# A fused attention and feed-forward kernel on one core: blocks of eight key tiles, three feed-forward banks, weight parts kept in memory

## The chip, the cores and the metric

The kernel runs on one core of one Trainium2 chip. The time is device microseconds (us) of one execution. A core has TensorE (PE: matmuls, with a queue for loading weights, PEld), VectorE (DVE), ScalarE (ACT), GpSimd (POOL) and SyncE (SP), whose queue issues most DMAs here. Matmuls write to eight PSUM banks of 128 x 512 fp32; DVE and ACT read them.

## The reference

Input x has 2048 tokens of 512 features; everything is fp32.

```python
xn = _layernorm(x, axis=-1)
s = _A_ref(xn, A_wqkv, A_wo)                          # 32 heads of 16: softmax(q k^T / 4) v, then @ wo
g = _silu(_B_ref(xn, B_w_gate, B_w_up, B_w_down))     # (silu(xn @ w_gate) * (xn @ w_up)) @ w_down, width 1792
return x + s * g
```

## The kernel before

**Precision.** Most matmuls use an fp32 operand split into a high and a low part of a rounded fp32 type (hi, then the rest), and three products of parts (high x high, high x low, low x high) stand for one. DVE makes the parts: a copy into the rounded type, then a subtraction.

**Stages.** A prologue normalises and transposes x, projects q, k and v for all heads and writes them to memory (`q_d`, `k_d`, `v_d`); the transposed input goes to `xt_d`. Then comes the attention stage, in which two streams of matmuls are woven together on PE:

- *Attention.* 32 units (a group of 4 heads times a quarter of the queries, 512), each with 16 key tiles of 128 keys. For a key tile there are two score pairs: two heads at a time, on the upper and lower 64 rows of PE at once, each to its own bank. ACT takes the exponential of the scores from PSUM into a tile `pr`. Then `values()` multiplies the exponentials with v, four heads side by side, into the bank `acc`. The units are cut into blocks of 2 to 6 key tiles. In block n the score pairs of block n are issued, with the values of block n - 1 in one run after its first two pairs.
- *Feed-forward* (`ffn`), in quarters of 512 tokens: 14 column tiles of gate and up ("gated tiles", 24 passes each), in two groups of seven; after a group, four token tiles of the down projection, 3 passes for each member of the group. `both()` issues a pass: two half-height matmuls at once, the upper 64 rows into `bankx`, the lower into `banky`. `fill(n)` issues the next n passes; the main loop calls it after every score pair, so that PE has work while ACT works on the scores.
- After the feed-forward the projection by `wo` (`project_out`) is issued by the same `fill`.

**PSUM.** `bankx`, `banky`, `acc`, two double banks `score` (a pair of heads each, emptied by one 128 x 1024 exponential) and one `spare`. The last pair of a block, and some pairs named in `SHARED`, put their second head into `spare`; there one half is emptied by a DVE copy (a *drain*), to be taken through the exponential from SBUF after the block's other exponentials (`kept_back`), or both by ACT one after the other.

**Order.** The order of every engine's instructions is that of the program text (manual schedule); `plan()` chooses sizes of blocks and numbers of passes after each score pair by a search over costs. Engines wait for each other by semaphores. All weight DMAs stand in SP's queue: every quarter loads gate, up and down weights anew (`load_gu`, `load_wd`) and splits them on DVE (`split_gu`, `split_wd`). `load_fx` replaces the transposed input of a quarter, 4.2 MB with both parts, after the last gated tile of the quarter before.

The lines that matter: the score matmuls L899 and their exponentials L902 and L910, drains L907, exponentials from SBUF L920, values L423, feed-forward passes L237, splits L198, L199, L208 and L209, reload of `fx` L215.

Of the kernel before, what the change touches and what calls it, by code (L numbers as in the profile page):

```python
# [22 lines left out]
H = 32  # L23
# [9 lines left out]
GROUPS = (slice(0, 7), slice(7, NF))  # L33
FG = 7
# [7 lines left out]
SIZES = (2, 3, 4, 5, 6)  # L42
LAST = (3, 3, 3, 3, 2, 2)
FIRST = (4, 1, 4, 0, 4, 1, 2, 4, 4)
EARLY = 2


SHARED = {
# [3 lines left out]
}  # L52
# [5 lines left out]
def plan():  # L58

    ends = [0]
    for i in range(2 * NB):
        nf = GROUPS[i % 2].stop - GROUPS[i % 2].start
        for n in [3 * DC] * nf + [3 * nf] * NT:
            ends.append(ends[-1] + n)

    ends = [n - ends[1] for n in ends[2:]]
    first = [(4, ends[0])]
    units = H // 4 * NB
    start, stop = sum(k for k, _ in first), (units - 2) * KT
    pace = (ends[-1] - ends[0]) / (stop - start)
    short = lambda k, n: 15 * len(SHARED[k, n][0]) if (k, n) in SHARED else 250 * max(0, 6 * (k - 1) - n)
    ways = {at: {} for at in range(start, stop + 1)}
    ways[start][ends[0]] = 0, None
    for at in range(start, stop):
        room = KT - at % KT  # L80
        for done, (cost, _) in ways[at].items():
            rem = next((n for n in ends if n > done), done) - done
            for k in SIZES:
                for n in [rem] + list(range(3, rem - 2)):
                    to = at + k, done + n
                    if not n or n > 6 * k + 6 or k > room or room - k == 1:
                        continue
                    if abs(to[1] - ends[0] - (to[0] - start) * pace) > 45:
                        continue
                    c = cost + 327 + short(k, n) + (650 if n == rem and k == 2 else 0) + abs(n - 4.1 * k) / 2  # L90
                    if to[1] not in ways[to[0]] or ways[to[0]][to[1]][0] > c:
                        ways[to[0]][to[1]] = c, (at, done, k, n)

    rest = [3 * (DT - 1)] * EARLY
    pairs = {4: (2, 2), 5: (3, 2), 6: (3, 3)}
    cost = lambda r: ways[stop - r][ends[-1]][0] + sum(short(k, n) for k, n in zip(pairs[r], rest))
    r = min((r for r in pairs if ends[-1] in ways[stop - r]), key=cost)
    middle, step = [], ways[stop - r][ends[-1]][1]
    while step:
        middle.insert(0, step[2:])  # L100
        step = ways[step[0]][step[1]][1]
    rest += [3 * DT] * (NT * (NB - 1))
    parts = []
    for k, n in first + middle + list(zip(pairs[r] + 2 * LAST, rest)):
        m = 2 * k - 2
        even = [n // m + (i < n % m) for i in range(m)]
        shared, behind = SHARED.get((k, n), ((), even))
        parts.append((k, shared, [0, 0, *behind]))
    parts[0] = 4, (), list(FIRST[1:])
    return parts  # L110
# [3 lines left out]
def tile_block(ctx: ExitStack, tc: tile.TileContext, x, wqkv, wo, w_gate, w_up, w_down, out):  # L114
# [3 lines left out]
    mm, act, dve, sp, pool = nc.tensor.matmul, nc.scalar.activation, nc.vector, nc.sync, nc.gpsimd  # L118
# [8 lines left out]
    o_d = dram.tile([DT, NB, P, TB], F32, name="o_d")  # L127
    s_d = dram.tile([1, TB], F32, name="s_d")
# [10 lines left out]
    banks = (bankx, banky)  # L139
# [45 lines left out]


    def load_gu(i):
        f = i % NF
        raw = two.tile([P, DC, P], F32, tag="gur", name="gur")
        for j, w in enumerate((w_gate, w_up)):  # L190
            sp.dma_start(raw[j * HALF:(j + 1) * HALF], w[:, f * P:(f + 1) * P].rearrange("(c p) f -> p c f", p=HALF))
        gu[i] = [raw]

    def split_gu(i):
        raw = gu[i][0]
        hi = two.tile([P, DC, P], F32R, tag="guh", name="guh")
        lo = two.tile([P, DC, P], F32R, tag="gul", name="gul")
        dve.tensor_copy(hi, raw)  # L198
        dve.tensor_sub(lo, raw, hi.bitcast(F32))  # L199
        gu[i] = (hi, lo)  # L200

    def load_wd(i):
        raw = one.tile([P, D], F32, tag="wdr", name="wdr")
        sp.dma_start(raw, w_down[(i % NF) * P:(i % NF + 1) * P])
        wdr[i] = raw

    def split_wd(f, i):
        dve.tensor_copy(wd[:, f, 0], wdr[i])  # L208
        dve.tensor_sub(wd[:, f, 1], wdr[i], wd[:, f, 0].bitcast(F32))  # L209
# [15 lines left out]
    kept, waiting = [], []  # L225

    def split_hidden():
        while kept:
            f, ga = kept.pop(0)
            dve.tensor_copy(hh[:, f, 0], ga)  # L230
            dve.tensor_sub(hh[:, f, 1], ga, hh[:, f, 0].bitcast(F32))  # L231

    halves = [slice(h * HALF, (h + 1) * HALF) for h in range(2)]

    def both(lhs, rhs, start, stop):
        for bank, h in zip(banks, halves):
            mm(bank, lhs[h], rhs[h], start=start, stop=stop)  # L237

    def store_gate(y, r):
        th = one.tile([P, D], F32, tag="th", name="th")  # L240
        act(th, y, AF.Tanh, scale=0.5)
        dve.scalar_tensor_tensor(y, th, 1.0, y, op0=ALU.add, op1=ALU.mult)
        pool.dma_start(g_d[r:r + P], y)


    def ffn(b):
        for grp, part in enumerate(GROUPS):
            nf = part.stop - part.start
            for f in range(nf):
                i = b * NF + part.start + f  # L250
                if i + 1 < NB * NF:
                    split_gu(i + 1)
                if i + 2 < NB * NF:
                    load_gu(i + 2)
                hi, lo = gu.pop(i)
                n = 0
                for c in range(DC):
                    for wt, j in ((hi, 0), (hi, 1), (lo, 0)):
                        both(wt[:, c], fx[:, j, c], n == 0, n == 3 * DC - 1)
                        n += 1  # L260
                        if n == 3 * DC:
                            th = one.tile([P, TB], F32, tag="th", name="th")
                            ga = two.tile([P, TB], F32, tag="ga", name="ga")
                            act(th, bankx, AF.Tanh, scale=0.5)  # L264
                            dve.scalar_tensor_tensor(ga, th, 1.0, bankx, op0=ALU.add, op1=ALU.mult)  # L265
                            dve.scalar_tensor_tensor(ga, ga, 0.5, banky, op0=ALU.mult, op1=ALU.mult)
                            kept.append((f, ga))
                            waiting.append((f, i))
                            if now >= 0:
                                split_hidden()  # L270
                            if grp == 1 and f == nf - 1 and b + 1 < NB:
                                load_fx(b + 1, 0)
                                load_fx(b + 1, 1)
# [39 lines left out]
    def next_out(t):  # L313
# [3 lines left out]
        if t + 1 < DT:  # L317
            load_wo(t + 1)
# [698 lines left out]
```

## Time and profile before

| | |
|---|---|
| runs shown | 1396.76 and 1397.27 us, median 1397.01 |
| profiled execution: span, first to last instruction | 1394.9 us |
| PE / ACT / DVE busy in it | 1388.4 / 1108.9 / 689.8 us |
| first score to last values | 157.6 to 1382.7 us |
| exponentials: 128 x 1024 / 128 x 512 from PSUM / from SBUF | 743 / 336 / 226 |
| DMA | 149.16 MB, mean 107 GB/s |

What lies around the span is the difference of 2.1 us between it and the median. In the profile a row of the timeline is: start, length, engine, line, operation, out<-in, count, and in brackets the idle time before it with what ended it. L12 is line 12 of the kernel. Matmuls overlap and their ends are modelled, so the distance between starts is read, not the length.

### The profile page before, as it was taken

Reading aid. Unit: us, or ns where it says so; the run is one execution under the profiler, and the core shown is the slowest. Engines: PE = TensorE matmul, PEld = TensorE weight load, DVE = VectorE, ACT = ScalarE, POOL = GpSimd, SP = SyncE. Lnnn points to the kernel's source line nnn. Section 1 sums busy time; section 2 is a strip of 40 time slices with the busy share of each in tenths; the row PEclk is TensorE's granted clock in tenths of the full one; section 3 lists DMA queues with packets and bytes.
Section 4 is the critical chain, followed back from the end, with each engine's and each line's share of the span. In section 5 each row is a group of like instructions: output and inputs, shape, how many; then the busy total and the mean of one; then the engine's idle time right before and its main releaser. Section 6 shows DMA issues by size and latency. Waiting matters only on the chain.

```text
span 1394.9 us, 27065 instructions
## 1 busy us (share of the span) xinstructions
PE 1388.4 (100%) x11197; PEld 835.5 (60%) x11197; DVE 689.8 (49%) x1126; ACT 1108.9 (79%) x1516; POOL 89.5 (6%) x102
## 2 busy tenths in 40 slices
PE   9999999999999999999999999999999999999998
PEld 7788655556555655565565555656556556555554
DVE  5643454254534563455356434644455434554645
ACT  6733587888888888888888888888888888888774
POOL 4200100000000000000000000000000000000254
PEclk9999999999999999999999999999999999999999
DMA  7778541134453511245533302257234302233642
GB/s 237 263 250 268 144 115 43 35 69 111 107 129 81 134 43 36 51 103 111 128 83 102 98 13 51 67 134 156 65 81 113 79 15 59 61 83 105 196 151 107
DMA packets 128687, 149.16 MB, mean 107 GB/s; under 512 B 12593, under 2 KB 80689, under 8 KB 127790
## 3 DMA queue, kind: packets, MB, share of 16 engines
q1 hardware_dynamic: 123246, 126.72, 36.1%
q0 software_dynamic: 4880, 20.12, 3.9%
q8 instruction: 89, 1.46, 0.5%
q10 hardware_dynamic: 432, 0.52, 0.1%
q14 instruction: 40, 0.33, 0.1%
HBM read 107.46 MB, written 40.11 MB: 106 GB/s over the span
## 4 chain that ended last, share of the span: by engine, by line
PE 87%; ACT 1%; DVE 1%; issue 0%; DVEq 0%; ACTq 0%
PE acc L423 32%; PE bankx L237 29%; PE score L899 18%; PE banky L237 7%; PE spare L899 1%; ACT pr L902 0%; PE spare L955 0%; PE banky L955 0%; PE score L955 0%; DVE hh L231 0%; DVE pr L907 0%; DVE gul L199 0%; ACT pr L910 0%; DVE hh L230 0%; DVE y L962 0%
## 5 line engine op out<-in xcount | busy, mean ns | idle before, releaser
L902 ACT ACTIVATE pr<-score 128x1024 f32<-128x1024 f32 x743 | 722.5, 1029 | 95.8 <-PE score L899 86.2
L423 PE MATMUL acc<-pr,vst 128*17 128x512 f32 x4096 | 461.8, 593 | 0.0
L899 PE MATMUL score<-qst,kst 50*128 50x512 f32 x1767 | 406.9, 407 | 0.4 <-ACT pr L902 0.4
L237 PE MATMUL bankx<-fx,guh 64*128 64x512 f32 x896 | 303.3, 392 | 0.2 <-PEq L810 0.2
L237 PE MATMUL banky<-fx,guh 64*128 64x512 f32 x896 | 303.2, 392 | 0.0
L899 PEld LDWEIGHTS score<-qst,kst 50*128 50x128 f32 x1767 | 193.3, 184 | 161.9 <-ACT pr L902 66.0
L423 PEld LDWEIGHTS acc<-pr,vst 128*17 128x17 f32 x4096 | 110.3, 97 | 280.4 <-issue 272.3
L907 DVE COPY pr<-spare 128x512 f32<-128x512 f32 x166 | 114.3, 689 | 249.5 <-PE spare L899 188.5
L910 ACT ACTIVATE pr<-score 128x512 f32<-128x512 f32 x221 | 131.7, 596 | 100.2 <-PE spare L899 72.2
L237 PE MATMUL bankx<-wd,hh 64*128 64x512 f32 x672 | 197.1, 392 | 0.0
L237 PE MATMUL banky<-wd,hh 64*128 64x512 f32 x672 | 197.1, 392 | 0.0
L237 PEld LDWEIGHTS bankx<-fx,guh 64*128 64x128 f32 x896 | 167.0, 187 | 26.7 <-issue 0.9
L237 PE MATMUL banky<-fx,gul 64*128 64x512 f32 x448 | 175.3, 391 | 0.0
L237 PE MATMUL bankx<-fx,gul 64*128 64x512 f32 x448 | 175.3, 391 | 0.0
L237 PEld LDWEIGHTS banky<-fx,guh 64*128 64x128 f32 x896 | 167.1, 187 | 3.2
L265 DVE SCALAR_TENSOR_TENSOR ga<-th,bankx 128x512 f32<-128x512 f32 x56 | 38.5, 687 | 201.4 <-ACT th L264 201.4
L237 PEld LDWEIGHTS bankx<-wd,hh 64*128 64x128 f32 x672 | 125.2, 186 | 18.6
L237 PEld LDWEIGHTS banky<-wd,hh 64*128 64x128 f32 x672 | 125.2, 186 | 5.9
L920 ACT ACTIVATE pr<-pr 128x512 f32<-128x512 f32 x226 | 124.2, 633 | 0.0
L899 PE MATMUL spare<-qst,kst 50*128 50x512 f32 x281 | 118.0, 420 | 0.2 <-DVE pr L907 0.2
L237 PEld LDWEIGHTS bankx<-fx,gul 64*128 64x128 f32 x448 | 83.0, 185 | 13.5
L237 PEld LDWEIGHTS banky<-fx,gul 64*128 64x128 f32 x448 | 83.0, 185 | 1.6
(171 smaller groups left out, 1400.8 us busy)
## 6 DMA issues: line engine op xcount, KB each, us to landing
gur<-in_B_w_gate_dram SPq DMA_DIRECT2D x56, 256.0 KB
gur<-in_B_w_up_dram SPq DMA_DIRECT2D x56, 256.0 KB
wdr<-in_B_w_down_dram SPq DMA_DIRECT2D x56, 256.0 KB
kst<-k_d SPq DMA_DIRECT2D x192, 64.0 KB
qst<-q_d SPq DMA_DIRECT2D x192, 64.0 KB
fx<-xt_d SPq DMA_DIRECT2D x24, 512.0 KB
q_d<-parts SPq DMA_DIRECT2D x16, 512.0 KB
k_d<-parts SPq DMA_DIRECT2D x16, 512.0 KB
```

What stands on the lines that cost most here:

```text
L237: mm(bank, lhs[h], rhs[h], start=start, stop=stop)
L265: dve.scalar_tensor_tensor(ga, th, 1.0, bankx, op0=ALU.add, op1=ALU.mult)
L423: mm(acc[h * 32:h * 32 + DH + 1], v[:, kt % CT, h * (DH + 1):(h + 1) * (DH + 1)], probs[2 * i + h // 2][:, h % 2], start=kt == 0, stop=kt ...
L899: mm(spare if apart and h else room[:, h], k[r, j, kc * P:(kc + 1) * P], q[r, j], start=True, stop=True)
L902: exps.append(act(pr, room, AF.Exp, scale=0.25))
L907: dve.tensor_copy(pr[:, h], src)
L910: exps.append(act(pr[:, h], src, AF.Exp, scale=0.25))
L920: exps.append(act(part, part, AF.Exp, scale=0.25))
```

## The change

- Attention: `plan()` has no search any more. Every unit is two blocks of eight key tiles, except the first (4, 6, 6) and the last (8, 4, 4): 66 blocks. Fills are spread evenly.
- Scores: four single banks, `score[0..3]`; pair j uses banks 2j and 2j + 1. There is no `spare`. Each half gets an exponential of its own from PSUM, or a drain to `pr` by DVE with the exponential later from SBUF; which one, a clock kept in the program text decides (`clock`, `charge`, `free`), with at most ten drains in a block of eight. Values take key tiles without a drained half first.
- Feed-forward: a third bank `bankz` (taken from `spare`). A unit of passes (`unit`) writes its upper half into one bank at once and its lower half, seven passes later (`LAG`), into the next; banks rotate. Groups are 5, 5 and 4 tiles.
- Weights: in the first quarter the parts are made as before and also written to memory (`gu_d`, `wd_d`); the later three quarters load the parts.
- Chores of DVE (splits) wait in a list and are put into the order when the program's clock finds DVE free.

```diff
-GROUPS = (slice(0, 7), slice(7, NF))
-FG = 7
+GROUPS = (slice(0, 5), slice(5, 10), slice(10, NF))
+FG = 5
+LAG = 7
...
+TILES = 17
...
-SIZES = (2, 3, 4, 5, 6)
-LAST = (3, 3, 3, 3, 2, 2)
+OPENING = (4, 6, 6)
+SIZES = (8, 8)
+CLOSING = (8, 4, 4)
+KEPT = {8: 10, 6: 6, 4: 3}
+PASS, QUAD, TURN, SEEN = 232, 860, 450, 200
...
     def load_gu(i):
...
+        b, f = divmod(i, NF)
+        if not b:
+            gu[i] = rows_of(F32)
+            came["gu", i] = clock["pe"]
+            for j, w in enumerate((w_gate, w_up)):
+                sp.dma_start(gu[i][j * HALF:(j + 1) * HALF], w[:, f * P:(f + 1) * P].rearrange("(c p) f -> p c f", p=HALF))
+        elif i % 3 == 2:
+            gu[i] = [rows_of() for _ in range(2)]
+            for w in range(2):
+                sp.dma_start(gu[i][w].bitcast(F32), gu_d[f, :, w])
+        else:
+            both = weights()
+            sp.dma_start(both.bitcast(F32), gu_d[f])
+            gu[i] = [both[:, w] for w in range(2)]
...
-    def both(lhs, rhs, start, stop):
-        for bank, h in zip(banks, halves):
-            mm(bank, lhs[h], rhs[h], start=start, stop=stop)
...
+    def follow():
+        i, lhs, rhs, start, stop, done = lagging.pop(0)
+        mm(banks[i], lhs, rhs, start=start, stop=stop)
...
+    def unit(terms, lead, lag, others=()):
...
+            mm(banks[first % 3], lhs[halves[0]], rhs[halves[0]], start=start, stop=stop)
+            if stop:
+                empty[first % 3] = NEVER
+                lead(first % 3)
+            lagging.append((second % 3, lhs[halves[1]], rhs[halves[1]], start, stop, lag))
+            if len(lagging) > LAG:
+                follow()
+            advance(PASS)
...
+            if i % NF == NF - 1 and b + 1 < NB:
+                load_fx(b + 1, 0)
+                load_fx(b + 1, 1)
...
-    def fill(n):
+    def blocked():
+        return not queue or queue[0][0] is not None and ready[queue[0][0]] < DT
+
+    def fill(upto, most=MOST):
         nonlocal given
-        while n > 0 and not blocked():
+        while given < upto and most and not blocked() and (now < 0 or upto == total or not waits()):
...
-    spare = spool.tile([P, 512], F32, name="spare")
-    score = [spool.tile([P, 2, 512], F32, name=f"score{i}") for i in range(2)]
+    banks.append(spool.tile([P, 512], F32, name="bankz"))
+    score = [spool.tile([P, 512], F32, name=f"score{i}") for i in range(4)]
...
+                room = score[2 * j:2 * j + 2]
+                while n > 2 and given < goal + sum(parts[n:]) and clock["pe"] < max(free[2 * j:2 * j + 2]) and not blocked():
+                    if waits():
+                        break
+                    fill(given + 1)
+                clock["pe"] = max(clock["pe"], *free[2 * j:2 * j + 2])
                 for h in range(2):
                     r = slice(h * HALF, h * HALF + NROW)
-                    mm(spare if apart and h else room[:, h], k[r, j, kc * P:(kc + 1) * P], q[r, j], start=True, stop=True)
+                    mm(room[h], k[r, j, kc * P:(kc + 1) * P], q[r, j], start=True, stop=True)
                 pr = ppool.tile([P, 2, TB], F32, tag="pr", name="pr")
...
+                for h in range(2):
+                    there = clock["pe"] + SEEN
+                    room_left = len(kept_back) < KEPT[size] * (n + 1) / (2 * size)
+                    if now and n > 1 and room_left and max(clock["dve"], there) + 608 < max(clock["act"], there) + 494:
+                        drain(pr[:, h], room[h])
+                        kept_back.append(pr[:, h])
+                        behind.add(n)
+                        free[2 * j + h] = clock["dve"] + 110
                     else:
-                        exps.append(act(pr[:, h], src, AF.Exp, scale=0.25))
+                        exps.append(act(pr[:, h], room[h], AF.Exp, scale=0.25))
+                        free[2 * j + h] = clock["act"] + 110
+                advance(PASS)
```

In the order of the changed kernel as built, ACT has 1456 exponentials from PSUM (128 x 512 each) and 592 from SBUF, DVE has 592 drains, SP has 168 weight DMAs as before.

More of the change, by code (lines that the diff above doesn't have):

```diff
@@ L77, in plan @@
[L77 to L108, printed above, removed]
@@ L249, in ffn @@
             for f in range(nf):
[L250 to L273, printed above, removed]
-                        if i and n == (DC if i > 1 else 3 * DC):
-                            if waiting:
-                                split_wd(*waiting.pop(0))
-                            load_wd(i)
-                        yield 3 * DC - n
@@ L868, in tile_block @@
         for now in range(begin[u], begin[u + 1]):
[L869 to L870 removed]
+            size, parts = blocks[now]
+            ended, kept_back, behind = None, [], set()
             tiles = range(kt, kt + size)
```

548 lines of the change are left out of this document (378 added, 170 removed), and 3 rows, old and new, of the table SHARED.

## The prediction

> **What bounds the kernel now.** I read the page's sums first, then stages, then single instructions in order of time.
>
> ```profile
> span 1394.9 us, 27065 instructions
> PE 1388.4 (100%) x11197; PEld 835.5 (60%) x11197; DVE 689.8 (49%) x1126; ACT 1108.9 (79%) x1516; POOL 89.5 (6%) x102
> PEclk9999999999999999999999999999999999999999
> ```
> ```profile
> 158.00:1382.00 1224.00, 1223.39 (x10438) 705.59 (x10440) 599.91 (x924) 1027.60 (x1376) 56.48 (x64) 1.00 0.36 89
> 0.00:145.00 145.00, 143.82 (x645) 114.51 (x647) 74.98 (x175) 77.06 (x134) 28.58 (x34) 1.00 0.81 254
> ```
> The columns of the second fence (the view by windows) are the stretch, its length, then busy time of PE, weight loads, VectorE (DVE), ScalarE (ACT), GpSimd, the granted clock, the DMA share and GB/s. PE is never idle, but ends of matmuls are modelled, so I look at their starts, at one change from scores to values and back (timeline of PE):
>
> ```profile
> 600.04 0.39 PE L237 MATMUL bankx<-fx,guh 64*128 64x512 f32 x1
> 600.27 0.39 PE L237 MATMUL bankx<-fx,gul 64*128 64x512 f32 x1
> 602.38 0.64 PE L899 MATMUL score<-qst,kst 50*128 50x512 f32 x4
> 602.95 4.49 PE L423 MATMUL acc<-pr,vst 128*17 128x512 f32 x40
> 607.37 0.49 PE L899 MATMUL score<-qst,kst 50*128 50x512 f32 x1
> 607.71 0.40 PE L237 MATMUL bankx<-fx,guh 64*128 64x512 f32 x1
> ```
> Two half-height matmuls run side by side (bankx and banky, or two heads' scores): one such pass each 0.23 us (600.04 to 600.27). I use 0.2335. The 40 value records are five key tiles. The chain of waits gives their slope:
>
> ```profile
> 663.22 1.84 PE acc L423 x16
> 670.72 3.56 PE acc L423 x32
> ```
> Two tiles more, 1.72 us more: 0.86 us a tile. Then a change costs 602.95 - (602.38 + 2 x 0.2335) = 0.10, plus 607.37 - (602.95 + 5 x 0.86) = 0.12, plus 0.34 - 0.2335 = 0.11: 0.33 us a block. The plan of before has 115 blocks. Its attention stage should take 512 tiles x 0.86 + (1024 score + 2150 feed-forward) passes x 0.2335 + 115 x 0.33 = 440 + 741 + 38 = 1219 us, and the stage lasts 1224 (158 to 1382). So PE waits for almost nothing: **only passes and changes of block can be saved**, and any new wait is paid in full.
>
> **The change, part by part.** The sum starts from this execution, 1394.9; the median shown is 1397.0, so 2.1 us lie around the span and are kept.
>
> *Blocks.* 115 become 66: 49 x 0.33 = **-16 us**. Passes and tiles are the same 2150 + 1024 and 512 (I counted them in the built order).
>
> *The last pair of a block.* Before, its second head goes to the bank `spare`, so that two engines empty it at once:
>
> ```profile
> 669.04 0.39 PE L899 MATMUL score<-qst,kst 50*128 50x512 f32 x1
> 669.05 0.39 PE L899 MATMUL spare<-qst,kst 50*128 50x512 f32 x1
> 669.47 0.69 DVE L907 COPY pr<-score 128x512 f32<-128x512 f32 x1 [2.09 <-PE spare L899]
> 669.86 0.18 PEld L899 LDWEIGHTS score<-qst,kst 50*128 50x128 f32 x2 [0.16 <-ACT pr L902]
> 669.98 0.75 PE L899 MATMUL score<-qst,kst 50*128 50x512 f32 x4
> 670.22 0.19 PEld L899 LDWEIGHTS score<-qst,kst 50*128 50x128 f32 x2 [0.18 <-DVE pr L907]
> ```
> A score issued at 669.04 is read from 669.47 (0.43 later), a drain on DVE lasts 0.69, and PE loads its next weights 0.06 after it ended: the bank is back after 1.18 us. ScalarE's row:
>
> ```profile
> 661.14 1.03 ACT L902 ACTIVATE pr<-score 128x1024 f32<-128x1024 f32 x1 [1.31 <-PE score L899]
> 662.07 0.60 ACT L910 ACTIVATE pr<-score 128x512 f32<-128x512 f32 x1
> 662.56 0.59 ACT L910 ACTIVATE pr<-spare 128x512 f32<-128x512 f32 x1
> 663.04 1.95 ACT L902 ACTIVATE pr<-score 128x1024 f32<-128x1024 f32 x2
> 670.18 1.15 ACT L920 ACTIVATE pr<-pr 128x512 f32<-128x512 f32 x2
> 671.22 1.94 ACT L902 ACTIVATE pr<-score 128x1024 f32<-128x1024 f32 x2
> ```
> One bank follows another after 0.48 (662.56 to 663.04), a double bank after 0.93, a second pass from SBUF after 0.52 (two in 1.04), and one bank lasts 0.60. So a pair whose halves are both left to ACT is back after 0.43 + 0.48 + 0.60 + 0.05 = **1.56 us**. The changed kernel has two pairs of banks and no spare. The next block's second score needs the banks of the last pair; between them stand the last fill (2 or 3 passes) and the next block's first score. With 3 that is 5 passes, 1.17 us; with 2, 0.93. In the built order, of 61 blocks of eight, 22 end with both halves on ACT and 3 passes: 22 x 0.39 = 8.6. 15 with 2: 15 x 0.63 = 9.4. 7 with one half drained and 2 passes: 7 x 0.25 = 1.7. Together **+20 us**. Behind the waiting score stand all values of the block, on PE, so nothing hides it.
>
> *Pairs inside a block.* A pair of banks is needed again two scores later: 1.40 us with 4 fills between, 1.63 with 5, 1.87 with 6. Pairs wholly on ACT: 45 with 4 fills, 129 with 5, 17 with 6. The 45 are late by 0.16: **+7**. The others are on time only if ACT and DVE are free when the score ends. 72 tanh of 0.48 stand in ACT's order; one pair in three is wholly on ACT, with 0.07 to spare at 5 fills, so they cost about 72 x 0.33 x 0.41 = 10. DVE has some 340 us of other work in the stage (600 less 226 drains of 0.69, less 127 of splits, plus 22 of regrouping, both below), 28% of it. A drain that meets a 0.69 us operation at a random point of it is late by 0.16 on average where its pair has 0.22 to spare (128 pairs with 4 fills) and by 0.04 where it has 0.45 (333 with 5): 0.28 x (128 x 0.16 + 333 x 0.04) = 10. Before shows no row for this; bounds are 0 (the order was laid out so that they never meet) and 40 (each meeting doubled by the backlog it leaves). I take **+15**.
>
> *Load of ACT and DVE.* 743 double exponentials become singles: ACT by these paces 1456 x 0.48 + 592 x 0.52 + 35 = 1042 us in the stage, where before has 743 x 0.93 + 336 x 0.48 + 226 x 0.52 + 35 = 1005. 85% of some 1225: not the bound on average, so 0 here; what it costs is the lateness above.
>
> The Trainium skill speaks against this part: ScalarE: Activation LUTs, What ACT_TABLE_LOAD costs, gives 186 ns plus 0.833 ns an element and 93 ns of overlap, 0.52 us a bank and 0.95 a double one. By that a wholly ACT pair would be back 0.05 later, 4 us more over the 82 late pairs; the trace's 0.48 decides.
>
> *Weight parts in memory.*
>
> ```profile
> L199 DVE TENSOR_TENSOR gul<-gur,guh 128x1024 fp32r<-128x1024 f32 x56 | 68.6, 1226 | 2.1
> L198 DVE CAST guh<-gur 128x1024 fp32r<-128x1024 f32 x56 | 38.3, 684 | 3.1 <-DVEq L810 3.1
> L209 DVE TENSOR_TENSOR wd<-wdr,wd 128x512 fp32r<-128x512 f32 x56 | 38.8, 693 | 1.9
> L208 DVE CAST wd<-wdr 128x512 fp32r<-128x512 f32 x56 | 23.4, 418 | 0.0
> ```
> DVE loses 42 of each 56: 3/4 of 169 = 127 us. It gains 366 drains x 0.69 = 253. No PE wait ended with these splits, so their going saves 0. Queue SP issues as many weight DMAs as before (168), but 99 MB in place of 44: about 146 GB/s over the span in place of 107.
>
> *Feed-forward banks and groups.* Three banks, the second half seven passes late, give the readers more time; PE waited for none, so 0. Three groups in place of two add 32 adds of `facc` on DVE, 22 us, counted in the 30%. But `fx` is reloaded (4.2 MB) nearer to its use:
>
> ```profile
> 376.00:380.00 4.00, 4.00 (x40) 1.45 (x34) 1.05 (x3) 2.83 (x5) 0.00 (x0) 1.00 1.03 207
> 392.00:396.00 4.00, 4.00 (x36) 1.85 (x34) 1.32 (x4) 3.46 (x6) 0.54 (x1) 1.00 1.07 228
> ```
> At some 205 GB/s, with DMA saturated, it takes 21 us; before has 84 feed-forward passes for it, the new order 41, with two runs of values about 29 us. One weight load of 1 MB and a store of 0.5 stand ahead: 28 us. Bounds 0 and 3 x 5; I take **+2**.
>
> *The end.* From block 59 fills are missing, because projections wait for attention output: six scores in a row (block 60), three at the end of 59. Six with nine halves on ACT: the sixth waits for five, 0.43 + 5 x 0.48 + 0.17 = 3.0 against 5 x 0.2335: 1.8. The end of 59 is late by 1.56 - 0.47 = 1.1, five lesser places by 0.16 to 0.5. That is 5; bounds 3 and 15 (if filler also waits for splits and loads there), and I take **+6**.
>
> *Prologue.* PE is busy 143.8 of 145.0, its work is unchanged: 0.
>
> Sum: -16 + 20 + 7 + 15 + 2 + 6 = +34, so 1429 us in the span, **1431 us**.
>
> **The rivals.** *Only the changes of block count*, the other side of the forecast: the four banks are separate, a first head's score may go as soon as its own bank is back (1.08 us by the same rows), and the second's lateness vanishes if PE is held for less than a pass. For it: in before, single banks at 669.98 were on time. Against: PE's matmuls start in order, so a held second head holds what follows. It decides if the real return is under 1.17 us for a pair on ACT. Price: 1397 - 16 = 1381, up to 1412 if half of the lateness stays.
>
> *ACT becomes the bound.* If singles come at 0.52 or meet more backlog, 85% becomes 91%, and late pairs pass their lateness on: the mid-block term 40 in place of 15, the end of the blocks 30: 1431 + 25 + 10 = 1466; from 1452 on.
>
> *Loads come late.* At 205 GB/s 28 us against 29 leaves nothing: if the reload or the 1 MB weight loads are late by 5 to 8 us at three boundaries, and queries behind them on SP too, 1431 + 20 = 1451. The change not doing what it says: the blocks and banks stand in the order, so no.
>
> **How the numbers follow.** Forecast 1431 (1412 to 1452): 0.52. Only changes of block, 1381 to 1412: 0.22. ACT the bound: 0.18. Late loads: 0.08. The range 1395 to 1464 leaves out about a tenth on each side. A measurement of this kernel tells about 2% (28 us) from no change: 1369 to 1425 holds the second case and the lower third of the first, 0.38; faster than 1369 would take 85 changes of block gone where 49 go, 0.01; slower 0.61.
>
> **What would show it.** Right: scores on PE with gaps of 0.4 to 0.6 us before a block's values, ended by ACT; value runs of eight tiles in 6.9 us plus 0.33; exponentials at 0.48; a run of six scores near the end ended by ACT. Wrong: no idle ahead of scores (second case); ACT over 95% busy (third); PE waiting for DMA at the first pass after an `fx` load (fourth). What would upset all is a pass that no longer takes 0.2335 us now that its halves belong to different tiles.

## The result, and the profile after

The changed kernel takes **1464.34 us** (two runs, 1462.45 and 1466.22) against 1397.01 before: 1.048 times as long (95% interval 1.0462 to 1.0502). The forecast was 1431. The profiled execution has a span of 1460.4 us, 65.5 more than before. Below are lines of the changed kernel's page (busy times, the row of PE in 40 slices and its clock), then the view of the clock by cores, of before and of after:

```profile
span 1460.4 us, 28049 instructions
PE 1430.8 (98%) x11197; PEld 904.3 (62%) x11197; DVE 802.3 (55%) x1384; ACT 1192.9 (82%) x2259; POOL 87.8 (6%) x102
PE   9999999999989999999999999999999999999898
PEclk9999999999999999999999999999999999999999
```
```profile
core 0: 1394.9 us, clock 0.999
```
```profile
core 0: 1460.4 us, clock 0.994
```

No engine is the bound by its share: ACT is at 82%. PE has the same 11197 matmuls, its busy share is 98% in place of 100, and its mean clock is lower by half a per cent, at most some 7 us of the span. In the row of 40 slices only three show PE below 9: one at 402 to 438 us and two near the end. So the loss lies in two kinds of places, and I measured both from the starts of PE's records: a block's length, from its third score to the next block's third score, less 0.2335 for each pass and score, 0.8585 for each tile and 0.325 for one change (the prediction's 0.86 and 0.33 with a digit more). What is left is called the block's *loss* below. Before, it was 7.1 us in all 115 blocks. After, it is 83.7 in 66:

| blocks (numbered from 0) | loss, us |
|---|---|
| 0 to 2 | 4.1 |
| 54 ordinary blocks, 3 to 58 without 14 and 44 | 39.5 (0.73 each) |
| 14 and 44, where a quarter's `fx` is reloaded | 8.2 and 5.5 |
| 59 to 65, the end | 26.3 |

Fewer changes give back 49 x 0.325 = 15.9. The first score comes 2.3 later (159.9) and 2.5 more lie behind the last values; why was not traced. 83.7 - 7.1 - 15.9 + 2.3 + 2.5 = 65.5, the whole difference.

**An ordinary block.** The timeline of PE at the end of block 20 of the changed kernel:

```profile
550.59 0.39 PE L369 MATMUL banky<-fx,gw 64*128 64x512 f32 x1
550.64 0.39 PE L350 MATMUL bankz<-fx,gw 64*128 64x512 f32 x1
553.62 0.39 PE L369 MATMUL banky<-fx,gw 64*128 64x512 f32 x1
553.70 0.39 PE L350 MATMUL bankz<-fx,gw 64*128 64x512 f32 x1
553.86 1.12 PE L1119 MATMUL score<-qst,kst 50*128 50x512 f32 x4
554.91 1.48 PE L625 MATMUL acc<-pr,vst 128*17 128x512 f32 x12
```

Two things are to be seen. The two scores (four halves) and the turn to the values take 554.91 - 553.86 = 1.05 us. Before, the same stretch was 0.67, from the scores at 669.98, which the prediction shows, to

```profile
670.65 0.62 PE L423 MATMUL acc<-pr,vst 128*17 128x512 f32 x4
```
This block of before is one of its longer ones: the median there is 0.58, that of the changed kernel's ordinary blocks 1.07. And the halves of a pass do not start together any more: 0.05 apart at 550.6, 0.08 at 553.6. In the rows of before that the prediction shows, those of the pair at 669.04 start 0.01 apart. One half of PE runs behind the other, and the lag stays until the values, which need both. Split in this way the 39.5 us of the ordinary blocks are: first halves late inside the block 9.9, second halves lagging inside the block 9.0, last pair 4.9 (first half) + 10.6 (second), and a turn to the values of 0.425 in place of 0.339, 4.6. Waits of PE for a score's bank end on ACT for the most part (view of waits, the columns are us, times, longest):

```profile
PEld score L1119 <- ACT pr L139: 87.1, 195, 5.2
PEld score L1119 <- DVE pr L145: 13.4, 31, 3.4
```

(Before, the first of these was 66.0 us in 164. These are waits of PE's queue for weight loads; part of each lies beside matmuls that still run, so their sums are no loss.)

**Block 14.** The chain of waits of the changed kernel, and the stretches around it (view by windows, columns as in the prediction):

```profile
411.56 0.61 SPq L313
412.21 20.24 DMA fx<-xt_d
432.48 1.51 DMA qst<-sh_d
434.08 1.19 PE score L1119 x3
435.27 8.53 PE acc L625 x64
```
```profile
412.00:428.00 16.00, 16.00 (x141) 10.13 (x134) 9.44 (x15) 12.39 (x24) 0.00 (x0) 1.00 1.07 204
428.00:432.00 4.00, 0.43 (x3) 0.00 (x0) 0.36 (x1) 4.00 (x9) 0.00 (x0) 0.94 0.99 184
432.00:436.00 4.00, 2.68 (x8) 0.94 (x12) 0.00 (x0) 3.20 (x6) 0.00 (x0) 0.50 0.04 10
436.00:440.00 4.00, 4.00 (x32) 0.94 (x28) 0.00 (x0) 1.60 (x3) 0.00 (x0) 0.70 0.00 0
```

The reload of `fx` takes 20.24 us at 204 GB/s (I had 21). No feed-forward pass waits for it: the next unit's queries (`qst`), issued on SP after it, come after it, and a score waits. PE idles some 4.8 us, and behind the idle the granted clock is 0.50, then 0.70: 64 value matmuls take 8.53 us in place of 6.99.

**The end.** The chain there runs through GpSimd (mul, add, store of an output tile), 1.28 us each:

```profile
1366.19 1.28 POOL y L569
1367.55 1.28 POOL gw L570
1368.84 0.28 issue
1369.14 0.58 POOL out_dram L571
1369.71 2.99 issue
1372.75 1.27 POOL y L569
```

### The profile page after: what moved, and what is told of

Read it like the earlier page. It is cut to its first block, busy times and chain, and to the rows that moved or that the text cites. A ratio compares the mean times of both kernels' runs of the same rounds, so it can differ in the third digit from the quotient of the medians.

```text
span 1460.4 us, 28049 instructions
## 1 busy us (share of the span) xinstructions
PE 1430.8 (98%) x11197; PEld 904.3 (62%) x11197; DVE 802.3 (55%) x1384; ACT 1192.9 (82%) x2259; POOL 87.8 (6%) x102
## 4 chain that ended last, share of the span: by engine, by line
PE 78%; issue 3%; DMA 3%; DVE 2%; POOL 2%; ACT 1%; SPq 0%; POOLq 0%; DVEq 0%; ACTq 0%
PE acc L625 28%; PE score L1119 19%; PE bankz L369 7%; PE bankx L369 6%; PE banky L369 6%; PE banky L350 4%; PE bankz L350 4%; PE bankx L350 3%; DMA fx<-xt_d 3%; POOL gw L570 1%; ACT pr L139 1%; POOL y L569 1%; DVE pr L145 1%; DVE facc L113 0%; SPq L313 0%
## 5 line engine op out<-in xcount | busy, mean ns | idle before, releaser
L139 ACT ACTIVATE pr<-score 128x512 f32<-128x512 f32 x1456 | 781.8, 608 | 168.4 <-PE score L1119 133.4
L145 DVE COPY pr<-score 128x512 f32<-128x512 f32 x592 | 401.6, 687 | 524.4 <-PE score L1119 512.9
L1119 PE MATMUL score<-qst,kst 50*128 50x512 f32 x2048 | 539.3, 414 | 16.0 <-ACT pr L139 7.9
L139 ACT ACTIVATE pr<-pr 128x512 f32<-128x512 f32 x592 | 314.9, 635 | 1.5 <-DVE pr L145 1.5
L369 PE MATMUL bankx<-fx,gw 64*128 64x512 f32 x366 | 111.4, 395 | 0.0
L369 PE MATMUL bankz<-fx,gw 64*128 64x512 f32 x360 | 109.2, 393 | 1.9 <-PEq L1018 1.9
L350 PE MATMUL banky<-fx,gw 64*128 64x512 f32 x366 | 110.2, 393 | 0.0
L350 PE MATMUL bankx<-fx,gw 64*128 64x512 f32 x360 | 107.4, 392 | 0.0
L369 PE MATMUL banky<-fx,gw 64*128 64x512 f32 x294 | 90.0, 395 | 0.0
L350 PE MATMUL bankz<-fx,gw 64*128 64x512 f32 x294 | 88.6, 392 | 0.0
L350 PE MATMUL bankz<-wd,hh 64*128 64x512 f32 x240 | 72.6, 392 | 0.0
L369 PEld LDWEIGHTS bankx<-fx,gw 64*128 64x128 f32 x366 | 66.4, 186 | 5.7 <-issue 0.3
L369 PE MATMUL bankz<-wd,hh 64*128 64x512 f32 x222 | 69.6, 399 | 0.0
L350 PEld LDWEIGHTS bankx<-fx,gw 64*128 64x128 f32 x360 | 66.9, 186 | 3.0 <-DVE ga L113 0.2
L350 PE MATMUL bankx<-wd,hh 64*128 64x512 f32 x222 | 67.5, 392 | 0.0
```

The costliest lines, as they stand in the source:

```text
L139: return nc.scalar.activation(out, *args, **named)
L145: return nc.vector.tensor_copy(out, src)
L350: mm(banks[i], lhs, rhs, start=start, stop=stop)
L369: mm(banks[first % 3], lhs[halves[0]], rhs[halves[0]], start=start, stop=stop)
L1119: mm(room[h], k[r, j, kc * P:(kc + 1) * P], q[r, j], start=True, stop=True)
```

## The experiments

All but e11 start from the changed kernel, whose 1464.34 us were taken once, ahead of them. The kernel before ran beside each experiment and took 1396.6 to 1397.1. In the diffs, `...` stands for lines left out.

**e1: the queries ahead of the reload.** In the program `load_q` and `load_shift` of the next unit move to the head of a unit's first block:

```diff
+            if u and now == begin[u] and u + 1 < units:
+                load_q(u + 1)
+                load_shift(u + 1)
             if now < 2:
...
-            if now == begin[u] + (not u) and u + 1 < units:
+            if not u and now == 1:
```

> Edit: the query and shift loads of the next unit stand at the head of SP's queue at the start of a unit's first block, ahead of the reload of fx; before they stood behind it. Theory (queries behind the reload): the block at the first boundary (26.87 us long, 8.24 over its own passes, tiles and one change) and the one at the third (24.15 us, 5.52 over) fall to the 0.7 over of an ordinary block, so 1464.3 - 7.5 - 4.8 = 1452; with the clock back in the values behind them, 1450 to 1454. Rival (the reload of fx itself is what comes late): the queries come early, the first feed-forward pass of the next unit waits the same 5 to 8 us, and the time stays within 3 us of 1464. Second rival: the weight loads that now stand behind the queries come late, 1460 to 1470 with new waits on the weight loads.

Measured: 1453.68 us (1453.49 to 1454.77), 10.7 less. Block 14 loses 0.87, block 44 0.83. The stretch that stood still is full, and the clock with it:

```profile
428.00:432.00 4.00, 4.00 (x33) 2.37 (x32) 2.12 (x4) 3.67 (x9) 0.00 (x0) 1.00 1.06 199
```

DMA is as busy as it was; only the order in SP's queue is different. Shown: the queries behind the reload were the cause, not the reload.

**e2: two buffers for y.**

```diff
-            box.append(one.tile([P, D], F32, tag="th", name="y"))
+            box.append(two.tile([P, D], F32, tag="ga", name="y"))
```

> Edit: y of an output tile takes one of two rotating buffers in place of the single th. Theory (the single buffer holds the last third of the projection back: it is held some 6.3 us from the first half's pass through the seven passes of lag to GpSimd's multiply and add): the waits of VectorE for GpSimd's multiply, 13.0 us in 7, vanish, and the last blocks (61 to 64, 16 us over their own work) lose 8 to 10, so 1454 to 1456. Rival (the six passes given at a time are what they wait for, or the readers of the output tile on VectorE and GpSimd): less than 3 us, 1461 to 1465.

Measured: 1461.73 us (1461.29 to 1462.18), 2.6 less, while the changed kernel's two runs differ by 3.8. Blocks 62 and 63 fall from 2.5 and 3.7 to 1.7 and 0.7, but block 60 rises by 1.7 and 61 by 0.6. The rise is not the edit's: e1, without it, has the same 6.3 and 9.5 there, and block 60 stands at 4.6 or 6.3 from one execution to the next. The single buffer was one wait of several; the rival holds for most of it.

**e3: the last pair always over two engines.**

```diff
-                    if now and n > 1 and room_left and max(clock["dve"], ...
+                    final = n == 2 * size - 1
+                    if now and n > 1 and (final and h or not final and room_left and max(clock["dve"], ...
```

> Edit: in the last pair of every block the second half always goes to VectorE and the first to ScalarE, so that two engines empty it. Theory (the pair left wholly to ScalarE is back only after 1.56 us, where the next block's second score needs it after 0.93 to 1.17): 44 blocks lose their lateness, 20 us by the prediction's term, of which 3 x 0.25 x 7 stays where only two fills are left, so 1464 - 15 to 20 = 1444 to 1449. Rival (the ordinary blocks' 41 us come from inside the blocks, not from their last pair): the time falls by less than 6 us, or rises where VectorE's other work is pushed back.

Measured: 1469.14 us (1466.29 to 1471.14), 4.8 more. The last pairs' 15.5 us became 14.9 (6.8 by first halves, 8.1 by second), so the edit did not remove what it was meant to remove: by the prediction's rows a half drained by DVE is back after 1.18 us at best, and needed after 0.93 to 1.17. The end rose to 35.9. This says nothing yet on the last pair's price; e8 and e11 do.

**e4: e1, e2 and e3 together.**

> Edit: the three edits together: queries ahead of the reload, two buffers for y, last pair of every block on two engines. If the causes are separate, the gains add up: 12 + 9 + 17 = 38, 1426, still slower than before (1397) by the mid-block term and the scores without fills near the end. If they hide one another (the end of the blocks and y's buffer both hold the last blocks), 5 to 10 less: 1432.

Measured: 1452.53 us (1451.19 to 1453.77). Only e1's gain stays.

**e5: the gates' loads on GpSimd's queue**, with e1 and e2.

```diff
-        sp.dma_start(gt[t], g_d[rows[t]])
-        sp.dma_start(xr[t], x[rows[t]])
+        pool.dma_start(gt[t], g_d[rows[t]])
+        pool.dma_start(xr[t], x[rows[t]])
```

> Edit: on the kernel with the queries first and two buffers for y, the loads of the gates and residual rows of the output tiles are issued on GpSimd's queue, which also issues the stores they wait for, in place of SP's. Theory (near the end the loads of the attention output, o_d, stand on SP behind loads that wait for GpSimd's stores, 29.4 us of SP's waiting in 8 times; VectorE then waits for their split, and the drains of the scores stand behind it): the wait of 5.0 us for the last score of block 61 goes and blocks 61 to 63 lose at most 4 us in place of 12, so 1453.7 - 2.6 - 8 = 1443. Rival (the attention output itself is late, stored and read back through memory after its own normalisation): block 61 still loses over 7, 1449 to 1453.

Measured: 1445.98 us (1443.96 to 1449.19). Blocks 61, 62 and 63 lose 6.2, 1.7 and 0.7, where with e1 alone they lost 9.5, 2.5 and 3.7. So 8 of the end's 28 were waits behind stores in SP's queue and y's buffer. What is left in block 61 is the rival's; the chain of waits of e5:

```profile
1349.68 0.72 DVE o L113
1350.42 2.00 DMA o_d<-o
1352.48 3.80 DMA fx<-o_d
1356.30 1.31 DVE wd L113
1357.63 0.69 DVE wd L113
1358.32 0.60 DVE y L113
1358.92 0.61 DVE pr L145
1359.58 0.50 PE score L1122
```

The last attention output goes to memory and back (5.9 us); DVE stands at its split, and the drain of a score (`pr`) stands behind the split on DVE.

**e6: without the second passes** over drained halves, with e1.

```diff
-                exps.append(act(pr, pr, AF.Exp, scale=0.25))
+                charge("act", 65 + 0.838 * columns(pr))
```

> Left out, on the kernel with the queries first: the 592 second passes of ScalarE over halves that VectorE drained (their exponential is missing from the output), 315 us of ScalarE; the order on every engine stays. Theory (a pair's return is late by its own two exponentials and by what stands right ahead of it; ScalarE's total does not matter): ScalarE falls from 82% to 61% and the time by less than 6 us, 1448 to 1454. Rival (ScalarE is the bound, its backlog runs through the blocks): the 40 us that the ordinary blocks lose fall below 15, so 1425 to 1430.

Measured: 1454.22 us (1452.77 to 1455.07), the same as e1, and the page:

```profile
PE 1429.6 (98%) x11197; PEld 902.1 (62%) x11197; DVE 803.5 (55%) x1384; ACT 894.5 (62%) x1667; POOL 87.9 (6%) x102
```

298 us less work on ACT give nothing: the ordinary blocks still lose 39.3. ACT is not the bound; these passes lie beside the values, as ACT's row behind block 20 of the changed kernel shows (ten of them from 554.32 to 559.62, the values from 554.91).

**e7: 96 blocks in place of 66**, with e1: `SIZES = (6, 5, 5)`, and limits of drains to match, `KEPT = {8: 10, 6: 7, 5: 6, 4: 5}`. With these sizes a part of the output is not what the reference has (which order they upset was not traced); each engine's matmuls and exponentials are as many as in e1.

> Edit, on the kernel with the queries first: 96 blocks in place of 66 (the inner pairs of eight become 6, 5 and 5 tiles). Theory (each change of block costs 0.33 us and each block's last pair its lateness, wherever it stands, 0.29 here): 30 x (0.33 + 0.29) = 18.6 more, less 0.09 a change for 60 inner blocks if the longer turn to the values (0.42 where before has 0.33) belongs to eight tiles, 1453.7 + 18.6 - 5.4 = 1467. Rival (the lateness comes of long blocks, in which the backlog grows to the end; blocks of five and six lose next to nothing, as in the kernel before): 1453.7 + 10 - 35 = 1429.

Measured: 1487.89 us (1483.18 to 1489.93), 34 more than e1, of which 30 x 0.325 = 9.8 are the changes. A block loses as much as one of eight did: 0.43 in its last pair (0.29 in blocks of eight) and 0.13 inside (0.35). The turn to the values takes 0.424 in blocks of five and six also, so it does not belong to eight tiles, as I had thought possible. The rival falls: the lateness goes with the blocks' ends. The end, which loses 28 in e1, has other sizes here too, and part of the excess over 1467 is its; the rest of that excess is open.

**e8: fills between a block's first and second score**, with e1.

```diff
...
-        some = [0, 0]
-        for _ in range(2 * k - 2):
+        some = []
+        for n in range(2 * k):
+            if n == 1:
+                some.append(0)
+                continue
```

> Edit, on the kernel with the queries first: each block's feed-forward passes are shared out over 15 places in place of 14, the new one between the block's first and second score, so that the last pair of the block before is needed again two or three passes (0.47 to 0.70 us) later. Theory (the last pair's lateness, 15.5 us over 54 ordinary blocks, 4.9 by its first half and 10.6 by its second, which lags): it goes, and the other pairs get 0.17 pass less each, which costs some 4: 1453.7 - 11 = 1443. Rival (ScalarE's and VectorE's work is late as a whole, so the lateness moves to the pairs inside): 1452 to 1458.

Measured: 1450.64 us (1448.52 to 1455.68), 3.0 less than e1. The end of block 20 of e8:

```profile
553.96 0.39 PE L353 MATMUL bankz<-fx,gw 64*128 64x512 f32 x1
553.97 0.60 PE L1125 MATMUL score<-qst,kst 50*128 50x512 f32 x2
554.51 1.48 PE L628 MATMUL acc<-pr,vst 128*17 128x512 f32 x12
```

The score's halves follow the passes at their pace and the values come 0.54 after the first. Over 53 ordinary blocks (all but 6) the last pair's lateness is nearly gone (15.4 in e1, 0.6 here) and the turn is 0.344 again (4.3 less): so the last pair cost **some 19 us**, close to the prediction's term. The gain did not stay. Inside the blocks 12 more are lost, where the passes that went to the new place are missing, and in blocks 18 and 48 the clock fell behind an idle of 1.05 us (below), 3.5 each.

**e9: a bank made late**, on e5.

```diff
+                if n == 8 and now in range(18, 58):
+                    for _ in range((0, 0, 2, 0, 3, 0, 5, 0)[now % 8]):
+                        nc.scalar.activation(pr[:, 0], room[0], AF.Exp, scale=0.25)
```

> Added, on the kernel of e5 (1446.0): in 15 ordinary blocks (every second one from 18 to 54) the exponential of the ninth score's first half is done 2, 3 or 5 times more on ScalarE, the same values again, so that the bank comes back about 1.0, 1.5 or 2.5 us late by the paces of 0.48 and TensorE idles so long, five blocks of each. Theory (a late bank costs what it is late): 5 x (1.1 + 1.5 + 2.6) = 26 more, 1472, and each block loses its idle time and no more. Rival (the granted clock falls behind an idle of over 1 us, as behind the idle ahead of block 59 in the changed kernel, where passes took 0.43 in place of 0.23 for some 4 us, but not each time): of the 15 blocks about half lose some 2 us beyond their idle, so 1472 + 15 = 1487, with a granted clock near 0.985.

Measured: 1481.24 us (1475.65 to 1481.77), between the two. The five blocks with idles of 0.5 to 0.9 us lost 0.8 to 1.5 more than in e5, the five with 1.1 to 1.3 lost 1.4 to 1.7, and of the five with 2.2 to 2.6 one lost 2.9 and four 4.3 to 4.7. Two of these last, by the timeline of PE, and the four us behind each:

```profile
587.00 0.50 PE L1122 MATMUL score<-qst,kst 50*128 50x512 f32 x2 [2.47 <-ACT pr L139]
747.65 0.98 PE L1122 MATMUL score<-qst,kst 50*128 50x512 f32 x2 [2.48 <-ACT pr L139]
749.49 0.62 PE L350 MATMUL bankx<-fx,gw 64*128 64x512 f32 x1
749.92 0.62 PE L350 MATMUL bankx<-fx,gw 64*128 64x512 f32 x1
```
```profile
587.00:591.00 4.00, 4.00 (x33) 3.24 (x35) 2.97 (x5) 3.93 (x9) 0.00 (x0) 1.00 0.33 72
747.60:751.60 4.00, 3.95 (x21) 2.94 (x23) 1.98 (x3) 2.66 (x5) 0.00 (x0) 0.71 0.00 0
```

The same idle, and once the clock stays at 1.00, once it is 0.71 and passes are 0.43 apart.

**e10: the last tanh of the feed-forward later**, on e5: `later(clock["dve"] + 2500, gate)` in place of 110.

> Edit, on the kernel of e5: the last tanh of the feed-forward (on facc, ahead of the output tiles) are given to ScalarE 2.4 us later in the program's clock. Theory (in block 59 the tanh waits 1.3 us for VectorE, whose queue holds 6 us of splits and copies, and the exponentials stand behind it on ScalarE, so that TensorE idles 1.8 us): the block loses 2 in place of 4.5, 1443 to 1444. Rival (VectorE's queue itself holds the drains back there): no change within 1 us, 1445 to 1447.

Measured: 1445.88 us (1444.37 to 1449.81): no change, and PE still idles 1.80 us in block 59. The tanh was not what held it.

**e11: the kernel before without `spare` for the last pair.**

```diff
-                apart = last_pair or n in shared
+                apart = n in shared and not last_pair
```

> Edit, on the kernel before: the last pair of each block is emptied by one double exponential on ScalarE from its own pair of banks; the spare bank is not used for it. Nothing else is changed. Theory (a last pair that is left to ScalarE is back after 0.43 + 1.03 + 0.05 = 1.51 us and is needed after 1.17 where three passes stand between): 0.34 in each of some 113 blocks, 38 us, 1435, less what the fewer VectorE copies give back. Rival (a late last pair is caught up by the second half, or lies beside the turn to the values): under 6 us, 1397 to 1403.

Measured: 1449.49 us (1449.19 to 1450.18), 52.9 more (ratio 1.0377, 1.0359 to 1.0394). The timeline of PE of e11:

```profile
689.92 0.39 PE L899 MATMUL score<-qst,kst 50*128 50x512 f32 x2
690.72 0.49 PE L899 MATMUL score<-qst,kst 50*128 50x512 f32 x2 [0.41 <-ACT pr L902]
691.14 1.05 PE L423 MATMUL acc<-pr,vst 128*17 128x512 f32 x8
```

The second score comes 0.80 after the first in place of 0.23. Over 101 blocks it is late by 0.428, and the turn takes 0.426 in place of 0.339: 0.51 a block. I had 0.34. The rival is out.

**e12: all mends**: e5 with the edits of e8 and e10.

> The mends together: queries first, two buffers for y, gates on GpSimd's queue, the last tanh later, and fills between a block's first and second score. Theory (they add up, with the lateness inside the blocks and the blocks without fills near the end left): e5's 1446 less 2 for the tanh, less 3 as fills between the first two scores gave, 1441, over 1397 still. If the idles of 1 us in blocks 18 and 48 of that order no longer take the clock down with them, 7 less, 1434.

Measured: 1437.69 us (1437.13 to 1441.0), ratio 1.0292 (1.0274 to 1.0309). The best of these, and still 41 us slower than the kernel before. Blocks 18, 33 and 48 still lose 4.4, 4.3 and 3.0 and the end 16.9.

**e13: the late splits on GpSimd**, on e5: `pool.tensor_copy` and `pool.tensor_sub` for the parts of `wo` and of the attention output.

> Edit, on the kernel of e5 (1446.0): the splits of the output weights and of the attention output, which come near the end, are made by GpSimd in place of VectorE. Theory (blocks 59 and 60, which lose 4.5 and 6.3, and block 61, 6.2, wait for drains and exponentials that stand behind these splits on VectorE): VectorE loses some 30 operations of 0.42 to 0.69 us there, the three blocks lose 4 to 8 less, 1438 to 1442. Rival (those blocks lose because passes are missing, as parts of the attention output come late, and scores follow scores): GpSimd makes a split slower than VectorE, so the parts come later still, and the time stays or rises, 1445 to 1455.

Measured: 1452.96 us (1450.55 to 1457.79), 7 more. Block 61 falls from 6.2 to 0.7, so what it lost did stand behind the splits on DVE. But GpSimd takes 0.62 and 1.27 us for a split's copy and subtraction, where DVE takes 0.42 and 0.69, and the loss comes back elsewhere: blocks 59, 60, 62 and 63 rise by 1.6, 4.1, 3.1 and 2.2. So DVE's queue alone does not make the end. Passes that can't be issued have a part in it: in e5's timeline of PE, block 60 has six scores in a row without a pass:

```profile
1328.66 4.01 PE L1122 MATMUL score<-qst,kst 50*128 50x512 f32 x12
```

At 0.2335 each they would start within 1.2 us. This move to a slower engine does not tell the two apart for blocks 59 and 60.

**e14: nineteen idles of 1.6 to 2.1 us**, on e5: as e9, four times more, in every second block from 18 to 54.

> Added, on the kernel of e5: in 19 ordinary blocks (every second one from 18 to 54) the exponential of the ninth score's first half is done 4 times more, so that TensorE idles 1.7 to 2.0 us in each, between the 1.2 us after which the clock fell in none of five and the 2.2 to 2.6 after which it fell in four of five. Theory (the fall depends on where an idle lies against a window that runs on by itself, so that the share grows with the length): it falls in 5 to 12 of the 19, each 1.6 us more; 1446 + 19 x 1.9 + 8 to 19 = 1490 to 1501. Rival (a fixed length decides): in none, 1482, or in all, 1512.

Measured: 1500.73 us (1495.79 to 1505.7). Eleven blocks lost 2.1 to 2.5 more than in e5, eight (18, 24, 26, 32, 34, 42, 46, 52) 3.7 to 4.0. The stretches behind the idles of blocks 18 and 20:

```profile
508.00:512.00 4.00, 4.00 (x26) 3.26 (x26) 1.75 (x3) 2.75 (x6) 0.00 (x0) 0.66 0.00 0
551.00:555.00 4.00, 4.00 (x37) 3.73 (x34) 2.37 (x4) 3.79 (x8) 0.00 (x0) 1.00 0.02 6
```

Eight of nineteen, as the theory has it; no fixed length decides: behind 1.61 us in block 46 the clock fell, behind 1.99 in block 54 it did not. The trace's records of the granted clock show the window itself. The falls of e14 begin at 509.27, 635.56, 676.52, 802.82 us and so on, and every distance between two of them is a whole multiple of 3.413 us; so it is in each run here with more than one fall. Cut into such windows, the idle of block 18 lies in one, that of block 20 in two:

```profile
505.86:509.27 3.41, 1.58 (x15) 1.25 (x15) 1.15 (x3) 3.25 (x7) 0.00 (x0) 1.00 0.22 89
509.27:512.68 3.41, 3.41 (x20) 2.75 (x18) 2.06 (x3) 2.26 (x5) 0.00 (x0) 0.50 0.00 0
546.82:550.23 3.41, 2.15 (x19) 1.72 (x16) 2.60 (x5) 2.96 (x6) 0.00 (x0) 1.00 0.75 250
550.23:553.64 3.41, 2.94 (x25) 2.69 (x27) 1.29 (x2) 3.26 (x7) 0.00 (x0) 1.00 0.14 58
```

What goes with the fall is the number of matmuls that start within one window, where 29 half-height ones fit. From block 3 to 58 of e8, e9, e12 and e14 the clock fell 17 times, always behind a window with at most 14 starts, and never behind 15 or more; two windows of e14 (blocks 40 and 54) had 14 and 12 and no fall. The idles of 1.05 us in e8 fit this, since few matmuls start around them: 6 and 8 in the windows of blocks 18 and 48, 20 and 15 in those of block 33, where it did not fall.

**e15: the mends that helped, with e13's splits.**

> The mends that helped, with the splits of e13: queries first, two buffers for y, gates on GpSimd's queue, fills between a block's first and second score, late splits on GpSimd. If e13's theory holds: the 1437.7 of all mends less 4 to 8, 1430 to 1434; if not, 1437 to 1447.

Measured: 1446.80 us (1444.11 to 1449.06), as e13 said: the end loses 24.8.

## Why the prediction was right and wrong

| term of the sum | predicted | measured |
|---|---|---|
| 49 fewer changes of block | -16 | -15.9 |
| last pair of a block | 20 | 20.1 (15.5, and 4.6 by the turn) |
| pairs inside a block | 7 + 15 | 18.9 |
| reload of `fx` (blocks 14 and 44) | 2 | 13.7 |
| the end (blocks 59 to 65) | 6 | 26.3 |
| first three blocks | 0 | 4.1 |
| ahead of the first score, behind the last values | 0 | 4.8 |
| what the blocks of before lose | 0 | -7.1 |
| rest of the ordinary blocks | 0 | 0.5 |
| sum | 34 | 65.4 |

*Blocks.* Right: e7's 30 further blocks cost their 0.325 each beside their lateness.

*Last pair.* Right in its size (e8: some 19 when it is taken away), not in one reason. I wrote that in the kernel before "two engines empty it at once". e3 gave it two engines and won nothing. What counts is the bank: with `spare` the half that comes back late is one that the next score does not need, and e11 shows what that was worth, 53 us in the kernel before. The size came out of two errors that met: the first halves are late by 4.9 and the second only lag, 10.6, less than the 20; but the turn to the values becomes 0.09 longer when the second score's weights have to wait for its bank (e11 shows the same step, e8 takes most of it away), which the sum did not have. That the two met at 20 was luck.

*Pairs inside.* Near in size, 18.9 for 22. The reasons given for it, meetings with a tanh and with DVE's other work, were not tested one by one; e6 only shows that the second passes on ACT are no part of it.

*Reload of `fx`, the step "28 us against 29".* The mechanism that I set against it came about, and the size failed: the load took 20.2 us, the passes did not wait, and the queries did. I had named them in the rival of late loads ("queries behind them on SP too") and charged nothing for them in the sum. e1 gives 10.7 back. The rival spoke of three boundaries; two were hit.

*The end.* This is the step of the prediction that failed most: its term of 6 us measured 26.3, above its own upper bound of 15. With the reload, 13.7 for 2, it makes up nearly the whole difference between the 34 us forecast and the 65.5 measured in the span. I counted six scores without passes and some late ends. Measured were: stores and loads of the output tiles that hold each other in SP's queue and in y's buffer (8 of 28 by e5), the trip of the attention output through memory with VectorE's queue standing behind it (block 61), and the scores without passes (blocks 59 and 60, 11 us in e5). My upper bound of 15 was for splits and loads; I left out who stands behind them on DVE. How the 11 us of blocks 59 and 60 divide stays open: e10 and e13 only say that neither the tanh nor the splits on DVE alone make them, and one fall of the clock is in them (block 60 of e5, at most 1.7 us).

*Weight parts and feed-forward banks.* Put at 0, and no wait of PE in the view of waits ended with a load of weights; the only loads there are those of the queries. DMA moved 140 GB/s on the mean, 146 were forecast.

*The clock.* I assumed 1.00 throughout. The mean of 0.994 costs at most some 7 us more than before, all of it inside the terms for blocks 14 and 44 and the end.

*The rivals.* "Only the changes of block count" assumed that the second half's lateness vanishes. The halves do run apart, which hides it for a moment, and it is paid at the values. "ACT becomes the bound" gave 1466 and is out by e6: the number was met by other causes.

## What to carry to other kernels

A spare bank for the last pair ahead of a long run is worth what it saves in every run: count the banks, not the engines that empty them. When a large reload moves, list what is issued behind it on the same queue, and price the first thing that is needed from there. Where PE never idled, price an idle at its length, and add a clock fall of 1.6 us where it may leave a window of 3.4 us with less than half of its matmuls: idles of 1.6 to 2.1 us did so in 8 of 19 cases here. And check whose drain stands behind an instruction that waits for a DMA.

## What the runs showed of the hardware

- *An idle of PE can cost more than its length.* Behind an idle of 1.6 to 2.1 us the granted clock fell in 8 of 19 cases (0.50 for 3.41 us, passes 0.43 apart), each 1.6 us more; behind 1.1 to 1.3 in none of 5 (e9), behind 2.2 to 2.6 in 4 of 5, behind 1.05 in blocks 18 and 48 of e8 (in block 33, 1.04, it did not; in e12 it fell in 18 and 33 and not in 48). The falls lie on a fixed beat of 3.413 us, and behind windows with at most 14 of 29 starts. The Trainium skill, TensorE: Matmul & The Clock Gate, section What's actually happening, says that the gate halves the clock after an idle window of about 3.4 us, and that the windows run on by themselves. The trace agrees on the half (0.50 behind the idle of block 14) and on the windows (the beat of 3.413 us, and the same idle of 2.47 or 2.48 us, once with the fall and once without); on the length it does not: idles well under 3.4 us were enough.
- *The two halves of PE run apart.* One half waits for its bank while the other goes on. From pass to pass the lag carried on was mostly up to 0.25 us, about one pass (0.31 at the first score behind block 12); in the last score ahead of the values, where no pass follows, the second half started up to 0.55 behind the first (block 29). The lag stays until a matmul that needs all rows. The Trainium skill, TensorEngine Tiling (Array Packing), section Key Properties, says that tiles operate independently; the starts at 553.62 and 553.70 agree.
- *The turn from scores to values takes 0.32 to 0.37 or 0.42 us.* It goes with the last score's weight load. Where that load stood at least 0.06 us ahead of its matmul, the turn was 0.31 to 0.37 (104 of 114 turns of before); where it waited for the bank and the matmul followed at once, 0.42 to 0.43 (the other 10, the one at 670.65 among them, 111 of 114 in e11 and all 54 of the changed kernel's ordinary blocks). In both cases the first load of the values came no sooner than 0.42 behind that load.
